# Weight chunks between two DMA queues, and the order of the first key matmuls, in a fused linear-attention and GeGLU kernel

## The chip, the cores and the metric

The kernel runs on one core of a Trainium2 chip. A time is the device time of one execution in microseconds, and the metric is the median over several executions; lower is better. The engines are named as in the profile: PE is TensorE (matmuls; PEld are its weight loads), DVE is VectorE, ACT is ScalarE, POOL is GpSimd and SP is SyncE, which here only issues DMAs. "SPq" and "ACTq" are instructions of SP's and ScalarE's queues that issue DMAs.

## What is computed

Two blocks work on the same input `x` (2048 rows of 640, bfloat16) and are mixed by a gate for each row. Block A is linear attention with 32 heads of 20, block B a GeGLU feed-forward net with 1728 hidden columns.

```python
g = sigmoid((x * gate_w).sum(-1, keepdims=True))
q, k, v = split(x @ wqkv)                      # 32 heads of 20 each
phi = lambda t: where(t > 0, t + 1, exp(t)) + 1e-6
pq, pk = phi(q), phi(k)
kv = einsum("bhsd,bhse->bhde", pk, v);  z = pk.sum(over s)
o = (pq @ kv) / (pq . z + 1e-6)
a = o @ wo
b = (gelu(x @ w_gate) * (x @ w_up)) @ w_down
out = g * a + (1 - g) * b
```

## The kernel before

**Tiling.** Rows are cut into 16 tiles of 128 and the 640 input columns into 5 chunks of 128 (`KC`). A product with a weight goes chunk by chunk: the transposed x tile (`xT[:, k, tile]`) is the stationary operand, the weight's chunk `k` the moving one, and 5 chunks add up in PSUM.

**Stages.** First come keys and queries of tiles 0 to 3 (`KM` at lines 445 to 458, `QM` at 460 to 473), with the feature map phi on ScalarE and VectorE behind them (`phi1`, `phi2`). Then come keys and queries of tiles 4 to 15 (`KQ`, line 532), then the sum over rows of phi(k) times x (`MM`, line 589), then the feed-forward net's first two products (`G`, line 689) with the attention's small products between them, and at the end the output tiles (`O_tile`, line 855).

**Who sets the order.** Every instruction goes through one planner (`P.op`), which appends it to its engine's list in program order and works out the semaphore waits from the tiles that it reads and writes. Each engine runs its list in order. Every load has a semaphore of its own. So the order of `KM` calls is TensorE's order, and the order of `load_...` calls is the order of issue on the queue that is named (`eng="sp"` unless said otherwise).

**The loads at the start.** Tile 0 of x is loaded as it is (`load_x(0)`) and transposed on TensorE by `T` (line 429), then copied by VectorE. Tiles 1 to 15 are transposed by the DMA itself (`load_xT`, line 352). The key weights come as five chunks of 160 KB (`load_wk`, line 349). Their issue on the two queues is:

| queue | order of issue at the start |
|---|---|
| SP | x tile 0, wk 0, transposed x tile 1, wk 3, wk 4, transposed x tiles 2 and 3, wq 0 to 4, transposed x tiles 4 to 15, then the bulk of x and the other weights |
| ScalarE | a tiny load (line 361), wk 1, wk 2, then the first Exp with its table load (line 372), then `gate_w` (line 374) |

**The first matmuls.** Warm-up matmuls on constants (`warm`, line 415) run until x tile 0 is there. Then tile 0 is transposed (lines 506 and 507), and the keys of tiles 0 and 1 are made chunk by chunk, alternating:

| step | what TensorE does (lines 509 to 517) |
|---|---|
| 1 to 3 | tile 0, chunks 0, 1, 2 |
| 4 to 6 | tile 1, chunks 0, 1, 2 |
| 7, 8 | tile 0, chunk 3; tile 1, chunk 3 |
| 9 | the gate column (`gate_col`, line 496): one small matmul of `gate_w` |
| 10, 11 | tile 0, chunk 4; tile 1, chunk 4 |

One step is two matmuls, 512 and 128 columns wide (lines 453 and 454). A step waits for its x tile and its weight chunk. Tiles 2 and 3 follow with all five chunks each (line 521), then the queries.

Of the kernel before, what the change touches and what calls it, by code (L numbers as in the profile page):

```python
# [162 lines left out]
def bass_gated_mix__linear_attn_block__geglu_ffn__prompt_kernel(  # L163
# [63 lines left out]
    with (  # L227
# [8 lines left out]
        with contextlib.ExitStack() as stack:  # L236
# [12 lines left out]
            def new_dma_key():  # L249
                k = "in%d" % dma_next[0]  # L250
                dma_next[0] += 1
                return k
# [16 lines left out]
            wk = wkq[:, :, 0:640]  # L269
# [40 lines left out]
            r_wk = [P.sb("wk%d" % k, R_WK + k * WW, R_WK + k * WW + 640) for k in range(KC)]  # L310
# [29 lines left out]
            def dma_in(dst, src, writes, reads=(), eng="sp"):  # L340
                P.op(eng, lambda e, dst=dst, src=src: e.dma_start(dst, src),
                     reads=reads, writes=writes, dma=new_dma_key())
# [3 lines left out]
            def load_x(i, eng="sp"):  # L346
                dma_in(x_aug[:, i, 0:640], A_x[0, i * 128:(i + 1) * 128, :], [r_xn[i]], eng=eng)

            def load_wk(k, eng="sp", after=()):
                dma_in(wk[:, k, :], A_wqkv[k * 128:(k + 1) * 128, 640:1280], [r_wk[k]], reads=after, eng=eng)  # L350

            def load_xT(i, after=()):
                P.op("sp", lambda e: e.dma_start_transpose(xT[:, :, i * 128:(i + 1) * 128],
                                                           A_x[0, i * 128:(i + 1) * 128, :]),
                     reads=list(after), writes=[r_xT[i]], dma=new_dma_key())

            def load_wq(k, eng="sp"):
# [4 lines left out]
                 writes=[P.res("touch")], dma=new_dma_key())  # L362
            load_x(0)
            load_wk(0)
            load_xT(1)
            load_wk(3)
            load_wk(4)
            load_wk(1, "act")
            load_wk(2, "act")

            zero = nc.const_aps.tensor(0.0, (128, 1), F32)
            P.op("act", lambda e: e.activation(eg[:, 0:1], zero, ACT.Exp), writes=[r_eg[0]])
# [15 lines left out]
            for c in range(NHC):  # L388
# [9 lines left out]
                 reads=[r_ones], writes=[r_ident])  # L398
# [16 lines left out]
            def warm(count, n):  # L415
                def fn(e):
                    last = None
                    for w in range(count):
                        last = e.matmul(ps[:, 4, 0:n], one_l, one_r[:, 0:n], start=True, stop=True)
                    return last  # L420
                P.op("pe", fn, writes=[bank[4]])
# [4 lines left out]
            def slot(n):  # L426
                return SLOTS[n % 4]
# [17 lines left out]
            def KM(n, ks):  # L445
                i = seq[n][1]
                b0, b1 = slot(n)

                def fn(e):
                    last = None  # L450
                    for k in ks:
                        lhs = xT[:, k, i * 128:(i + 1) * 128]
                        e.matmul(ps[:, b0, :], lhs, wk[:, k, 0:512], start=(k == 0), stop=(k == KC - 1))  # L453
                        last = e.matmul(ps[:, b1, 0:128], lhs, wk[:, k, 512:640],  # L454
                                        start=(k == 0), stop=(k == KC - 1))
                    return last
                P.op("pe", fn, reads=[r_xTa[i] if i < NXN and ks == [0] else r_xT[i]] + [r_wk[k] for k in ks],
                     writes=[bank[b0], bank[b1]])
# [37 lines left out]
            def gate_col():  # L496

                P.op("pe", lambda e: e.matmul(ps[:, 7, 0:5], gw_sb, ident[:, 0:5], start=True, stop=True),
                     reads=[r_gw, r_ident], writes=[bank[7]])
                P.op("dve", lambda e: e.tensor_copy(wq[:, :, 640:641], ps[:, 7, 0:5].unsqueeze(2)),  # L500
                     reads=[bank[7]], writes=[r_gcol])
# [4 lines left out]
            T(0, [0], 7)  # L506
            T(0, [1, 2, 3, 4], 6)
            warm(2, 128)
            for k in range(3):
                KM(0, [k])  # L510
            for k in range(3):
                KM(1, [k])
            KM(0, [3])
            KM(1, [3])
            gate_col()
            KM(0, [4])
            KM(1, [4])
# [48 lines left out]
            for i in range(NQ, NT):  # L566
                KQ(i)
                if i == 4:
                    late_constants()
            P.op("dve", lambda e: e.tensor_scalar(gg, eg, 0.5, 0.5, ALU.mult, ALU.add),  # L570
                 reads=r_eg, writes=[r_g])
            P.op("dve", lambda e: e.tensor_scalar(omg, eg, -0.5, 0.5, ALU.mult, ALU.add),
                 reads=r_eg, writes=[r_omg])
# [7 lines left out]
                 reads=[r_omg], writes=[r_od], dma=new_dma_key())  # L581
# [44 lines left out]
            def ME(g):  # L626
# [6 lines left out]
                for c in cs:  # L633
# [8 lines left out]
                 reads=r_pk[0:2], writes=[r_tmp[0]])  # L642
            for i in range(2, NT):
                P.op("dve", lambda e, i=i: e.tensor_tensor(zacc, zacc, pk[i], ALU.add),  # L644
                     reads=[r_tmp[0], r_pk[i]], writes=[r_tmp[0]])
# [283 lines left out]
```

## Time and profile before

| what | value |
|---|---|
| median of 7 executions | 273.81 us (273.47 to 275.66) |
| the profiled execution, its own time | 273.41 us |
| its span, first to last instruction | 272.1 us |
| TensorE's granted clock | 1.000 |
| PE busy in 0.8 to 3.2 us / 3.2 to 4.4 / 4.4 to 5.55 | 2.38 of 2.40 / 0.73 of 1.20 / 0.97 of 1.15 us |
| PE busy in 7.6 to 15.9 us / 15.9 to 48.4 | 8.30 of 8.30 / 32.50 of 32.50 us |
| PE busy in 48.4 to 80 us / 80 to 270 | 31.60 of 31.60 / 190.00 of 190.00 us |

The span is counted from the first instruction. The time of an execution is somewhat longer than its span, because it holds what lies before the first and behind the last instruction. The rows on PE come from a view that gives the busy time of each engine in chosen stretches. In that view a stretch is followed by its length and then by the busy time of PE, PEld, DVE, ACT and POOL, with the number of instructions in brackets. A group such as `L453 PE MATMUL ps<-pool` is the matmul of line 453 that reads SBUF (`pool`, the kernel's one large tensor there) and writes PSUM (`ps`).

### The profile page before, as it was taken

The numbers are of one execution on the slowest core, as the hardware profiler recorded it, in microseconds if no ns is written. First come the engines' busy times: TensorE is split into PE (matmuls) and PEld (weight loads), VectorE is DVE, ScalarE is ACT, GpSimd is POOL, SyncE is SP. The second block draws the span as 40 slices with busy tenths as digits, with TensorE's granted clock in tenths as the row PEclk, the third lists the DMA queues.
The fourth block names the chain that finished last, engine by engine and source line by source line (L and its number), as shares of the span: only waits on it lengthen the run. The fifth ranks groups of instructions, "written<-read, shape, count | busy, mean of one in ns | idle before, by whom it ended". The sixth has DMA issues, their size and how long they took to land.

```text
span 272.1 us, 3442 instructions
## 1 busy us (share of the span) xinstructions
PE 268.7 (99%) x1367; PEld 127.5 (47%) x1367; DVE 140.7 (52%) x247; ACT 75.9 (28%) x132; POOL 30.0 (11%) x28
## 2 busy tenths in 40 slices
PE   7999999999999999999999999999999999999997
PEld 3555555544445444444444444444444444444444
DVE  1689898997333335999999999634110000000200
ACT  2455555210422453322222232224012122121021
POOL 5000000004140002243332421000000000000000
PEclk9999999999999999999999999999999999999999
DMA  7876999600300011614121221272031110110211
GB/s 193 199 117 124 326 398 390 165 3 19 65 13 2 23 50 51 201 26 49 27 48 32 41 51 24 60 244 81 5 81 35 41 39 19 39 41 19 58 58 41
DMA packets 42864, 23.78 MB, mean 87 GB/s; under 512 B 32223, under 2 KB 41439, under 8 KB 42719
## 3 DMA queue, kind: packets, MB, share of 16 engines
q1 hardware_dynamic: 42517, 23.22, 31.8%
q10 hardware_dynamic: 330, 0.33, 0.3%
q8 instruction: 11, 0.18, 0.3%
q14 instruction: 6, 0.05, 0.1%
HBM read 13.83 MB, written 2.63 MB: 60 GB/s over the span
## 4 chain that ended last, share of the span: by engine, by line
PE 97%; DMA 1%; SPq 0%; DVE 0%; issue 0%
PE ps L700 41%; PE ps L864 23%; PE ps L539 12%; PE ps L596 6%; PE ps L843 4%; PE ps L468 2%; PE ps L811 2%; PE ps L678 2%; PE ps L599 1%; PE ps L453 1%; DMA pool<-in_A_x_dram 1%; PE ps L824 1%; PE ps L721 1%; PE ps L739 0%; PE ps L469 0%; PE ps L454 0%
## 5 line engine op out<-in xcount | busy, mean ns | idle before, releaser
L700 PE MATMUL ps<-pool 128*128 128x512 bf16 x520 | 113.7, 379 | 0.0
L700 PEld LDWEIGHTS ps<-pool 128*128 128x128 bf16 x520 | 50.5, 98 | 60.0
L864 PE MATMUL ps<-pool 128*128 128x512 bf16 (+2 forms) x306 | 62.7, 367 | 0.0
L706 ACT ACTIVATE pool<-ps 128x512 f32<-128x512 f32 x52 | 31.0, 597 | 73.1 <-PE ps L700 73.1
L708 DVE TENSOR_TENSOR pool<-ps,pool 128x512 bf16<-128x512 f32 x52 | 34.7, 690 | 31.7 <-PE ps L700 30.4
L864 PEld LDWEIGHTS ps<-pool 128*128 128x128 bf16 x306 | 29.2, 98 | 33.5 <-issue 0.4
L847 DVE TENSOR_TENSOR pool<-ps,pool 128x512 bf16<-128x512 f32 x4 | 2.8, 692 | 61.5 <-PE ps L843 61.5
L539 PE MATMUL ps<-pool 128*128 128x512 bf16 (+1 forms) x180 | 32.7, 344 | 0.0
L754 POOL TENSOR_TENSOR pool<-pool 128x640 f32<-128x640 bf16 x16 | 22.4, 1405 | 73.0 <-DVE pool L756 66.1
L871 ACT ACTIVATE pool<-ps,pool 128x512 bf16<-128x512 f32 (+1 forms) x16 | 10.9, 680 | 68.6 <-PE ps L864 68.6
L539 PEld LDWEIGHTS ps<-pool 128*128 128x128 bf16 x180 | 17.5, 98 | 15.0
L558 DVE SCALAR_TENSOR_TENSOR pool<-ps,pool 128x128 bf16<-128x128 f32 (+2 forms) x36 | 21.7, 602 | 2.1
L549 ACT ACTIVATE pool<-ps 128x640 bf16<-128x640 f32 x24 | 16.9, 703 | 15.8 <-DVE pool L558 9.3
L596 PE MATMUL ps<-pool 128*128 128x512 bf16 x78 | 19.4, 379 | 0.0
L764 DVE TENSOR_TENSOR pool<-pool 128x640 bf16<-128x640 bf16 x16 | 13.2, 826 | 0.6
L762 DVE TENSOR_SCALAR pool<-pool 128x32 f32<-128x32 f32 x16 | 12.8, 800 | 0.6
L756 DVE TENSOR_REDUCE pool<-pool 128x32 f32<-128x640 f32 x16 | 13.0, 809 | 0.0
L644 DVE TENSOR_TENSOR pool<-pool 128x640 f32<-128x640 f32 x14 | 11.6, 825 | 0.5
L843 PE MATMUL ps<-pool 128*128 128x512 bf16 x52 | 11.6, 380 | 0.0
L646 POOL PARTITION_ALL_REDUCE pool<-pool x1 | 4.0, 3972 | 60.4 <-DVE pool L644 60.4
L596 PEld LDWEIGHTS ps<-pool 128*128 128x128 bf16 x78 | 6.9, 98 | 7.3
L555 DVE TENSOR_SCALAR pool<-pool 128x640 bf16<-128x640 bf16 x24 | 7.9, 327 | 1.7 <-ACT pool L549 0.4
(70 smaller groups left out, 123.9 us busy)
## 6 DMA issues: line engine op xcount, KB each, us to landing
out_dram<-pool SPq DMA_DIRECT2D x19, 128.0 KB, 1.7
pool<-in_B_w_gate_dram SPq DMA_DIRECT2D x1, 2080.0 KB, 14.5
pool<-in_B_w_up_dram SPq DMA_DIRECT2D x1, 2080.0 KB, 17.7
pool<-in_A_wqkv_dram SPq DMA_DIRECT2D x8, 160.0 KB, 3.1
pool<-in_A_x_dram SPq DMA_DIRECT2D x1, 1280.0 KB, 9.5
pool<-in_A_x_dram SPq DMA_DIRECT2D x1, 1120.0 KB, 6.6
pool<-in_B_w_down_dram SPq DMA_DIRECT2D x1, 1120.0 KB, 6.1
pool<-omg_row SPq DMA_DIRECT2D x1, 1024.0 KB, 5.0
```

The source lines that it names most:

```text
L539: last = e.matmul(ps[:, b + p, 0:c1 - c0], xT[:, k, i * 128:(i + 1) * 128], wkq[:, k, c0:c1], start=(k == 0), stop=(k == KC - 1))
L549: P.op("act", lambda e: e.activation(e_buf[m], ps_flat[:, o:o + 640], ACT.Exp), reads=banks, writes=[r_e[m]])
L558: P.op("dve", lambda e, c0=c0, c1=c1: e.scalar_tensor_tensor(dst[:, c0:c1], ps_flat[:, o + c0:o + c1], 1.0 + EPS, e_buf[m][:, c0:c1], ALU. ...
L596: last = e.matmul(ps[:, b, :], pk[i][:, c * 128:(c + 1) * 128], x_aug[:, i, 0:512], start=(i == 0), stop=(i == NT - 1))
L700: last = e.matmul(ps[:, b, :], w[:, k, fc * 128:(fc + 1) * 128], xT[:, k, j * 512:(j + 1) * 512], start=(k == 0), stop=(k == KC - 1))
L706: P.op("act", lambda e: e.activation(ge[n], ps[:, gb, :], ACT.Gelu_apprx_tanh), reads=[bank[gb]], writes=[r_ge[n]])
L708: P.op("dve", lambda e: e.tensor_tensor(hT[fc][:, j * 512:(j + 1) * 512], ps[:, ub, :], ge[n], ALU.mult), reads=[bank[ub], r_ge[n]], write ...
L754: P.op("pool", lambda e: e.tensor_tensor(tmp[n], pq[i], z_b, ALU.mult), reads=[r_pq[i], r_zb], writes=[r_tmp[n]])
L756: P.op("dve", lambda e: e.tensor_reduce(den[n], tmp[n].rearrange("p (h d) -> p h d", h=32), AX.X, ALU.add), reads=[r_tmp[n]], writes=[r_de ...
L764: P.op("dve", lambda e: e.tensor_tensor(pq[i].rearrange("p (h d) -> p h d", h=32), pq[i].rearrange("p (h d) -> p h d", h=32), den[n].unsqu ...
L843: last = e.matmul(ps[:, b, :], wd[:, fc, 512:640], hT[fc][:, j * 512:(j + 1) * 512], start=False, stop=(fc == NFC - 2), skip_group_check=True)
L864: last = e.matmul(ps[:, pb, 0:c1 - c0], lhs, rhs, start=False, stop=(q == len(rows) - 1), skip_group_check=True)
```

## The change

Chunk 3 of the key weights is issued from ScalarE's queue, behind chunks 1 and 2, and no longer from SP's. On SP chunk 4 follows the transposed x tile 1, and the transposed tiles 2 and 3 follow chunk 4. TensorE makes tile 0's chunks 0 to 3 and then tile 1's chunks 0 to 3; the gate column and the two chunks 4 follow as before. The parameter `after` of `load_wk`, which no call used, goes.

```diff
-            def load_wk(k, eng="sp", after=()):
-                dma_in(wk[:, k, :], A_wqkv[k * 128:(k + 1) * 128, 640:1280], [r_wk[k]], reads=after, eng=eng)
+            def load_wk(k, eng="sp"):
+                dma_in(wk[:, k, :], A_wqkv[k * 128:(k + 1) * 128, 640:1280], [r_wk[k]], eng=eng)
...
             load_x(0)
             load_wk(0)
             load_xT(1)
-            load_wk(3)
             load_wk(4)
             load_wk(1, "act")
             load_wk(2, "act")
+            load_wk(3, "act")
...
             warm(2, 128)
-            for k in range(3):
+            for k in range(4):
                 KM(0, [k])
-            for k in range(3):
+            for k in range(4):
                 KM(1, [k])
-            KM(0, [3])
-            KM(1, [3])
             gate_col()
             KM(0, [4])
             KM(1, [4])
```

## The prediction

> **What bounds the kernel now.** I read four views, in this order: the busy line and the chain's summary, the waits of TensorE, TensorE's timeline between 4.4 and 7.7 us, and the transfers of that stretch.
>
> ```profile
> PE 268.7 (99%) x1367; PEld 127.5 (47%) x1367; DVE 140.7 (52%) x247; ACT 75.9 (28%) x132; POOL 30.0 (11%) x28
> PE 97%; DMA 1%; SPq 0%; DVE 0%; issue 0%
> ```
>
> TensorE is busy for 268.7 of 272.1 us. Only 3.4 us are not matmul, whatever their cause. The waits of TensorE over the whole run are three:
>
> ```profile
> PE ps L419 <- PEq L914: 0.8, 1, 0.8
> PE ps L453 <- DMA pool<-in_A_wqkv_dram: 0.5, 1, 0.5
> PE ps L453 <- DMA pool<-in_A_x_dram: 0.2, 1, 0.2
> ```
>
> The last two sit at the keys (line 453), where the change is. The columns are the sum, the number of times and the longest. The 0.8 us is the start of the program, and about 1.7 us at the end are the last store; the change reaches neither. The timeline (start, duration, instruction, idle before):
>
> ```profile
> 4.99 0.38 PE L453 MATMUL ps<-pool 128*128 128x512 bf16 x1
> 5.20 0.22 PE L454 MATMUL ps<-pool 128*128 128x128 bf16 x1
> 5.59 0.39 PE L453 MATMUL ps<-pool 128*128 128x512 bf16 x1 [0.17 <-DMA pool<-in_A_x_dram]
> ...
> 7.25 0.38 PE L453 MATMUL ps<-pool 128*128 128x512 bf16 x1
> 7.47 0.22 PE L454 MATMUL ps<-pool 128*128 128x128 bf16 x1
> 7.57 0.39 PE L453 MATMUL ps<-pool 128*128 128x512 bf16 x1
> ```
>
> A step (one 512-wide and one 128-wide matmul of one chunk) takes 0.27 us from start to start (4.72, 4.99). So tile 0 has used chunks 0 to 2 at 5.26, and the next step starts at 5.59: a hole of 0.33 us, ended by the transposed x tile 1. Seven steps and the gate matmul then lead to 7.52, and tile 2's first step starts at 7.57: a second hole of 0.05 us. From there on TensorE doesn't pause. So the change can win at most 0.33 + 0.05 = 0.38 us, 0.14% of the time.
>
> The chain of waits, and SP's and ScalarE's queues in that stretch:
>
> ```profile
> 1.71 3.83 DMA pool<-in_A_x_dram
> 5.54 0.05 issue
> 5.59 0.39 PE ps L453
> ```
>
> ```profile
> 1.71 1.30 SPq L353 DMA_TRANSPOSE pool<-in_A_x_dram  x1
> 3.06 1.04 SPq L341 DMA_DIRECT2D pool<-in_A_wqkv_dram  x2
> 4.14 2.53 SPq L353 DMA_TRANSPOSE pool<-in_A_x_dram  x2
> ```
>
> ```profile
> 1.24 0.93 ACTq L341 DMA_DIRECT2D pool<-in_A_wqkv_dram  x2
> 2.20 1.28 ACT L372 ACT_TABLE_LOAD   x1 [2.20 <-issue]
> 2.28 0.56 ACTq L341 DMA_DIRECT2D pool<-in_gate_w_dram  x1
> ```
>
> Tile 1 is complete at 1.71 + 3.83 = 5.54. Its issue isn't touched by the change, but what shares the DMA engines with it is. The table by stage (last columns: granted clock, DMA share, GB/s) says how full they are:
>
> ```profile
> 3.50:4.00 0.50, 0.43 (x6) 0.25 (x4) 0.36 (x2) 0.20 (x1) 0.50 (x1) 1.00 1.04 369
> 4.00:4.50 0.50, 0.05 (x1) 0.08 (x2) 0.27 (x1) 0.00 (x0) 0.36 (x3) 1.00 1.24 309
> 4.50:5.00 0.50, 0.50 (x5) 0.25 (x6) 0.00 (x0) 0.00 (x0) 0.20 (x1) 1.00 1.31 239
> 5.00:5.50 0.50, 0.42 (x4) 0.09 (x2) 0.00 (x0) 0.00 (x0) 0.00 (x0) 1.00 0.91 228
> 5.50:6.00 0.50, 0.41 (x3) 0.27 (x4) 0.00 (x0) 0.00 (x0) 0.00 (x0) 1.00 0.98 334
> ```
>
> The engines are full from 3.5 to 6.0 us: here a transfer can be sooner only at another's expense. In the DMA view of 4.1 to 5.0 us, queue 1 (SP's; it holds tile 1's transpose) has 682 packets and queue 10 (ScalarE's) only 47. Tile 1 now has the engines nearly to itself once wk chunks 1 and 2 are through.
>
> **What the skill says.** The Trainium skill's page "DMA: Bandwidth & Descriptors", section "Issuing engines are not separate DMA queues", has it that transfers started by ScalarE and SP run on the same 16 engines and interleave, so a second issuer saves only issue time. The trace agrees: between 2.75 and 4.1 us queue 10 took 61.3% of the engines' time and queue 1 32.5%, 94% together. Its section "Queues, rings and completion order" says that an engine takes turns between the queues packet by packet, and that each queue's ring is drained in order. The trace shows both queues moving in that stretch, but no large SP transpose beside a ScalarE load; how they share is my main unknown. "TensorE: Matmul & The Clock Gate", section "HAM oscillation — how this bites in real kernels", warns of idle gaps of about 3.4 us and more; the gap here is 0.33 us and the clock stands at 1.00 in all stages, so I cost the clock at nothing.
>
> **The change part by part.** Completion times below are the trace's completion stamps of the single transfers: wk1 4.49, wk2 4.90, gate_w 5.20, x tile 1 5.54, wk3 6.28, wk4 6.72, x tile 2 7.53, x tile 3 8.36.
>
> ScalarE's queue. wk3 is issued third, at about 2.17 (after 0.93 us for two, which began at 1.24), and takes 0.46 us. That moves gate_w's issue from 2.28 to 2.74 and its completion from 5.20 to some 5.65 (0.45 for wk3 ahead of it); the gate matmul starts at 6.96, so 1.3 us of cover remain. The table load and the first Exp move by as much and end at 4.15 instead of 3.69; ScalarE's next work is at 7.45. Both cost nothing; gone the cover, each would cost its excess.
>
> SP's queue. wk4 is issued at 3.06, tile 2's transpose at 3.67 instead of 4.14, and all behind it about 0.47 sooner (POOL's queue is not touched). wk4 comes earlier than 6.72 and is needed at about 7.1.
>
> Order on TensorE. Tile 0's chunk 3 stands before tile 1's chunk 0. No matmul is added; 0.27 us of work moves into the 0.33 us hole, if wk3 is there. It adds a wait: behind KM(0, [3]) all tile 1 steps, the gate and everything else queue in order.
>
> When wk3 lands. It follows wk2 on its ring; wk1 to wk2 was 0.41 us, so 4.90 + 0.41 = 5.31 at best. At worst it waits until tile 1 is through: its bytes are 163,840 at 369 GB/s = 0.44 us, so 5.54 + 0.44 = 5.98. As turns are taken and its packets are the larger (1,280 bytes against the transpose's 256 or so), I take 5.35.
>
> What that does to tile 1. Bounds: 0 (if it isn't limited by the engines) and 0.44 us (if wk3 goes ahead of its remaining packets). The shares of 1.24 and 1.31 say that packets queue, so I take 0.38: tile 1 at 5.92, its first step at 5.97. By then tile 0's chunk 3 (5.40 to 5.67) is done and no longer in the way.
>
> Sum. From tile 1's first step there remain six steps instead of seven, and the gate: 6 x 0.273 + 0.05 = 1.69, against 7.57 - 0.05 - 5.59 = 1.93 before. Tile 2 can start at 5.97 + 1.69 = 7.66, against 7.57: +0.09 us. With the bounds: delay 0.44 gives 7.72, +0.15; delay 0.3 gives 7.58, no difference.
>
> Tile 2. Sooner issued, it's still behind the same bytes: everything through tile 2 (x tile 0 and 1, five wk chunks, tile 2) is the same sum of bytes, on engines that are full until 6.0. The half us after 6.5 has a share of 0.64 only, so tile 2 can gain some 0.1 of it in the likely case, and up to its 0.47 of issue if the engines weren't what held it. In the likely case it lands before 7.6 and isn't waited for.
>
> Behind. Tile 3 lands at 8.36 and is needed at 7.57 + 5 x 0.273 = 8.94. The wq chunks come last at 12.25, against first use at 10.30 + 8 x 0.273 = 12.48; they are issued 0.47 sooner. No new wait there. What is 0.09 late at 7.6 is 0.09 late at the end, as TensorE has no hole to absorb it.
>
> The profiled execution is 273.41 us, 272.1 of span and 1.3 around it. 273.41 + 0.09 = 273.5. It lies 0.40 under the median of 273.81, and I carry that over: 273.9.
>
> **Rivals.**
> A, the likely case: 273.75 to 273.95; the hole is filled but tile 1 is late by about as much.
> B, it works as arranged: tile 1 stays at 5.54 because wk3 finds gaps, and tile 2 profits from its sooner issue. wk3 at 5.31: tile 0's chunk 3 runs from 5.36 to 5.63, then 5.63 + 1.69 = 7.32, a gain of 0.25 (up to 0.38 with both holes closed): 273.4 to 273.6. For it speaks that tile 1's packets start some time after its issue, so part of wk3 could pass ahead; against it, the full engines.
> C, wk3 is late: its wait holds up tile 1, which is there. With 5.98, seven steps and the gate remain: 5.98 + 0.05 + 1.96 = 7.99, +0.42: 274.2.
> D, the other side: as C, but wk3 doesn't get its turn before the second transpose either. It decides from wk3 at 6.39 on (6.39 + 2.01 = 8.40, +0.83); 6.5 gives +0.94: 274.75. For it: wk3 was at 6.28 on SP, and nothing in this trace shows ScalarE's third load beside a transpose. Against: it is issued 0.9 us sooner, and wk2, in the same place, took 3.2 us from issue to landing.
>
> **How the numbers follow.** A 0.58, B 0.20, C 0.12, D 0.10. About 0.3%, 0.82 us, is what a measurement of this kernel can tell from no change. A, B and C lie within it, B's best (0.38) too. The seven times reach from 273.47 to 275.66, so a median may fall over either bound by itself: I put 0.04 on faster and 0.12 on slower, nearly all of it D. The predicted time is A's, 273.9. The range reaches from B (273.3) to D's lower end (274.7).
>
> **What would show it.** Right: the matmul after tile 0's third step starts near 5.4 with no long wait; tile 1's first step starts at 5.9 to 6.0 on x; tile 2's at 7.55 to 7.7 without a wait; DMA share in 4.0 to 5.5 no lower than now, queue 10 with over 150 packets between 4.1 and 5.0. Wrong: tile 1's transpose still complete near 5.54 and tile 2 before 7.3 (B), or a wait on wqkv longer than 0.3 us after 5.26 (C, D), or any wait of TensorE after 7.7, which I exclude.

## The result, and the profile after

| | kernel before | changed kernel |
|---|---|---|
| median | 273.81 us (30 executions, 273.46 to 275.66) | 275.20 us (12 executions, 274.62 to 276.69) |
| ratio, 95% interval | | 1.0061 (1.0046 to 1.0075) |
| the profiled execution, its span | 273.41, 272.1 us | 276.63, 275.3 us |

The change costs 1.4 us in the median. The forecast was 273.9, no difference, and its range ended at 274.7. The waits of TensorE in the changed kernel (sum, times, longest):

```profile
PE ps L453 <- DMA pool<-in_A_wqkv_dram: 1.1, 1, 1.1
PE ps L419 <- PEq L912: 0.8, 1, 0.8
PE ps L453 <- DVE pool L437: 0.3, 1, 0.3
```

The wait for x tile 1 is gone, and a longer one for a weight chunk stands in its place. The timeline of TensorE shows where, and a second thing:

```profile
4.39 0.59 PE L453 MATMUL ps<-pool 128*128 128x512 bf16 x1 [0.34 <-DVE pool L437]
4.76 0.31 PE L454 MATMUL ps<-pool 128*128 128x128 bf16 x1
4.87 0.63 PE L453 MATMUL ps<-pool 128*128 128x512 bf16 x1
...
5.83 0.31 PE L454 MATMUL ps<-pool 128*128 128x128 bf16 x1
7.21 0.61 PE L453 MATMUL ps<-pool 128*128 128x512 bf16 x1 [1.06 <-DMA pool<-in_A_wqkv_dram]
7.61 0.31 PE L454 MATMUL ps<-pool 128*128 128x128 bf16 x1
7.71 0.63 PE L453 MATMUL ps<-pool 128*128 128x512 bf16 x1
...
10.35 0.38 PE L453 MATMUL ps<-pool 128*128 128x512 bf16 x1
10.57 0.22 PE L454 MATMUL ps<-pool 128*128 128x128 bf16 x1
10.62 0.38 PE L453 MATMUL ps<-pool 128*128 128x512 bf16 x1
```

Tile 0's fourth step starts at 7.21. From its start on, seven steps and the gate lead to tile 2, as they did from 5.59 on in the kernel before, so 1.62 us are lost up to here. Then the steps themselves: from 7.71 on they take 0.53 us from start to start, from 10.35 on 0.27. The three steps ahead of the hole were slow already (4.39, 4.87, 5.41). Tile 2 starts at 10.62 (the last line) and not at 7.57, 3.05 us later: 1.62 from waiting and 1.43 from slow steps. The profiled execution is 3.22 us above the profiled one of before, so the start explains nearly all of it. It is one of the four slowest of the 12 executions (276.26 to 276.69); the other eight lie between 274.62 and 275.29, about where the wait alone would put them (an estimate: 273.41 + 1.62 = 275.03).

The chain of waits names the transfer (start, duration):

```profile
2.17 0.03 issue
2.19 4.97 DMA pool<-in_A_wqkv_dram
7.16 0.05 issue
```

wk3, issued at 2.19 on ScalarE's queue, arrived at 7.16; on SP's queue it had arrived at 6.28 although it was issued at 3.06. Tile 1's transpose suffers with it. The DMA view of the stretch in which both are on their way (size, time from issue to completion):

```profile
pool<-in_A_wqkv_dram ACTq DMA_DIRECT2D x1, 160.0 KB, 5.0
pool<-in_A_x_dram SPq DMA_TRANSPOSE x1, 5.6
```

Tile 1 took 5.6 us instead of 3.8: it is complete at 7.33 and not at 5.54. The table by stage, last columns granted clock, DMA share and GB/s, answers to the table shown of before:

```profile
4.00:4.50 0.50, 0.16 (x2) 0.14 (x2) 0.30 (x1) 0.18 (x1) 0.36 (x3) 1.00 1.11 283
4.50:5.00 0.50, 0.50 (x3) 0.23 (x2) 0.00 (x0) 0.00 (x0) 0.20 (x1) 1.00 1.42 158
5.00:5.50 0.50, 0.50 (x4) 0.12 (x3) 0.00 (x0) 0.00 (x0) 0.00 (x0) 1.00 1.11 134
5.50:6.00 0.50, 0.50 (x4) 0.06 (x2) 0.00 (x0) 0.00 (x0) 0.00 (x0) 1.00 1.24 138
```

The engines are as full as before (shares above 1.1), but from 4.5 us on they move 134 to 158 GB/s where they moved 228 to 334. In the kernel before, transposes alone filled the engines at 238 GB/s (7.1 to 7.3 us, share 1.06, every packet under 512 bytes), and the stretch of nearly only ordinary loads, 3.5 to 4.0, moved 369. The new rate lies below both, so it isn't sharing: sharing would give a rate between the two. So there are two theories to test. M, mixing: a transposing transfer of one queue and an ordinary one of another slow each other down on the same engines. C, clock: the longer hole in TensorE's work keeps its matmuls slow or makes them slow again. The rivals are that the order of the matmuls costs the time, that the sooner issues on SP do, or that any two queues do this.

### The profile page after: what moved, and what is told of

Read it like the earlier page. It is cut to its first block, busy times and chain, and to the rows that moved or that the text cites. A ratio compares the mean times of both kernels' runs of the same rounds, so it can differ in the third digit from the quotient of the medians.

```text
span 275.3 us, 3442 instructions
## 1 busy us (share of the span) xinstructions
PE 271.2 (99%) x1367; PEld 128.4 (47%) x1367; DVE 140.6 (51%) x247; ACT 76.0 (28%) x132; POOL 30.0 (11%) x28
## 4 chain that ended last, share of the span: by engine, by line
PE 97%; DMA 2%; ACTq 0%; DVE 0%; issue 0%
PE ps L698 41%; PE ps L862 23%; PE ps L537 12%; PE ps L594 6%; PE ps L841 4%; PE ps L453 2%; DMA pool<-in_A_wqkv_dram 2%; PE ps L468 2%; PE ps L809 2%; PE ps L676 2%; PE ps L597 1%; PE ps L822 1%; PE ps L719 1%; PE ps L737 0%; PE ps L454 0%; PE ps L469 0%
## 5 line engine op out<-in xcount | busy, mean ns | idle before, releaser
L698 PE MATMUL ps<-pool 128*128 128x512 bf16 x520 | 113.7, 379 | 0.0
L594 PE MATMUL ps<-pool 128*128 128x512 bf16 x78 | 19.4, 379 | 0.0
L841 PE MATMUL ps<-pool 128*128 128x512 bf16 x52 | 11.6, 379 | 0.0
L453 PE MATMUL ps<-pool 128*128 128x512 bf16 x20 | 7.9, 485 | 1.4 <-DMA pool<-in_A_wqkv_dram 1.1
```

The source lines that it names most:

```text
L594: last = e.matmul(ps[:, b, :], pk[i][:, c * 128:(c + 1) * 128], x_aug[:, i, 0:512], start=(i == 0), stop=(i == NT - 1))
L698: last = e.matmul(ps[:, b, :], w[:, k, fc * 128:(fc + 1) * 128], xT[:, k, j * 512:(j + 1) * 512], start=(k == 0), stop=(k == KC - 1))
L841: last = e.matmul(ps[:, b, :], wd[:, fc, 512:640], hT[fc][:, j * 512:(j + 1) * 512], start=False, stop=(fc == NFC - 2), skip_group_check=True)
```

## The experiments

**The changed kernel again, twice.** A second profile beside the next three runs, and a third with timing beside a later series.

> The changed kernel once more, for a second profile. Theory M (mixing): while wk chunk 3 on ScalarE's queue and the transposed x tile 1 on SP's queue are in flight together, the DMA engines move both far below their usual rate; tile 1 is complete at about 7.3 us and wk3 at about 7.1 us again (before: 5.54 and 6.28), and tile 0's chunk 3 starts at about 7.2. Theory C (clock): the long hole then also delays the moment at which TensorE's matmuls go from 0.54 us a step to 0.27 us a step; when that happens differs from run to run, so that this profile shows the fast steps either from before 5 us (then about 275.0 us) or from about 10 us on (then about 276.6 us). A rival that the clock is only an accident of that one profile, and always late in this kernel, expects 276.6 again.

> The changed kernel beside the other three, on the same chip: 275.2 with executions between 274.6 and 277; tile 1 complete at 7.2 to 7.4 us, wk3 at 6.9 to 7.6.

Tile 1 was complete at 7.40 and 7.94, wk3 at 7.57 and 7.89. The times were 277.10 (one execution) and a median of 276.99 (13 executions, 274.79 to 278.25; ratio 1.0094, 1.0068 to 1.0119). In both profiles the first steps were fast, so the guess that a profile is either fast from 5 us or slow up to 10 us was too simple. TensorE's timeline of the third profile:

```profile
4.70 0.38 PE L453 MATMUL ps<-pool 128*128 128x512 bf16 x1
4.91 0.22 PE L454 MATMUL ps<-pool 128*128 128x128 bf16 x1
6.00 0.39 PE L453 MATMUL ps<-pool 128*128 128x512 bf16 x1 [0.87 <-DMA pool<-in_A_wqkv_dram]
6.23 0.22 PE L454 MATMUL ps<-pool 128*128 128x128 bf16 x1
7.94 0.61 PE L453 MATMUL ps<-pool 128*128 128x512 bf16 x1 [1.49 <-DMA pool<-in_A_wqkv_dram]
8.34 0.31 PE L454 MATMUL ps<-pool 128*128 128x128 bf16 x1
```

Before the second hole a 512-wide matmul takes 0.38 us, behind it 0.61; TensorE was fast once more at 11.5. The table by stage of this profile, with the granted clock third from the end, has it as a clock:

```profile
7.00:7.50 0.50, 0.00 (x0) 0.00 (x0) 0.00 (x0) 0.00 (x0) 0.00 (x0) 1.00 1.09 268
8.00:9.00 1.00, 1.00 (x5) 0.45 (x6) 0.00 (x0) 0.00 (x0) 0.00 (x0) 0.50 1.24 316
11.50:12.00 0.50, 0.50 (x5) 0.29 (x4) 0.00 (x0) 0.50 (x2) 0.00 (x0) 1.00 0.96 213
```

The clock fell to one half at about 8.0 us, behind holes of 0.87 and 1.49 us close together, and rose at about 11.4. The second profile shows the same from 7.6 to 11.0, behind a wait of 0.79 us, some steps and a hole of 1.52. The first one reads 1.00 throughout although its steps were slow until 10.3, so in this view 1.00 doesn't prove fast steps.

**Order alone.** The queues of before, the new order of the matmuls:

```diff
-            for k in range(3):
+            for k in range(4):
                 KM(0, [k])
-            for k in range(3):
+            for k in range(4):
                 KM(1, [k])
-            KM(0, [3])
-            KM(1, [3])
```

> Only the order of the matmuls is changed, the queues are those of before. Theory M: tile 1 is complete at 5.5 us and wk3 at 6.3 us as before; tile 0's chunk 3 starts at 6.33 and holds up tile 1; seven steps and the gate remain, so tile 2 starts at 8.3 instead of 7.57: +0.7 us over before, 274.5, and more if the hole of 1.1 us makes the clock late. Rival (the order itself costs the whole 1.4 us): 275.2. Rival (order is harmless): 273.8.

274.19 us, 22 executions, against 274.01 of before beside it: ratio 1.0011 (0.9996 to 1.0027). The transfers were as before (tile 1 at 5.62, wk3 at 6.44), and tile 2 started at 8.43. The cost was smaller than expected: no difference that can be measured. A second profile of before, below, suggests why. Fast steps stayed fast here behind a hole of 0.97 us:

```profile
6.49 0.39 PE L453 MATMUL ps<-pool 128*128 128x512 bf16 x1 [0.97 <-DMA pool<-in_A_wqkv_dram]
```

**Queues alone.** The changed loads, the old order (the reverse of the diff above, made to the changed kernel).

> Only the queues are changed, the order of the matmuls is that of before. Theory M: the transfers are as in the changed kernel, tile 1 complete at about 7.3 us, so tile 1's first step starts at about 7.35 with seven steps to go, against 7.2 with seven steps to go in the changed kernel: 275.2 to 275.4, as slow as the whole change. Rival (the wait of tile 0's chunk 3 in front of tile 1 is what costs): tile 1 comes first again and the time is about that of before, 273.8 to 274.0.

276.55 us, 10 executions (274.84 to 278.5): ratio 1.0092 (1.0059 to 1.0125). Tile 1 was complete at 7.31, wk3 at 7.11. TensorE's waits in it:

```profile
PE ps L453 <- DMA pool<-in_A_wqkv_dram: 0.8, 1, 0.8
PE ps L453 <- DMA pool<-in_A_x_dram: 0.7, 1, 0.7
```

The first wait is for the weights of tile 0's first step, the second is the hole: with the old order TensorE waits for tile 1 instead of wk3, to the same effect. So the loads cost the time, and the order doesn't save it. The median lies above the forecast. In the profile (277.79 us) the steps took 0.53 us from the first one to about 12.2, which would explain it; the other executions weren't traced.

**The same loads with an ordinary tile 1.** In the changed kernel and in the kernel before:

```diff
-            load_xT(1)
+            P.op("sp", lambda e: e.dma_start(xT[:, :, 128:256],
+                                             A_x[0, 128:256, :].rearrange("s (k p) -> s k p", k=KC)),
+                 writes=[r_xT[1]], dma=new_dma_key())
```

> The changed kernel, but x tile 1 is loaded by an ordinary copy in pieces of 256 bytes into the same place instead of by a transposing DMA (the transpose of that tile is left out, so the keys and queries of tile 1 are of other numbers). Theory M, in the form that a transposing and an ordinary transfer disturb each other: with no transpose in flight until tile 2's, wk3 is complete at about 5.3 us and tile 1 by about 5.9, ordinary packets of 1,280 bytes keep their 55 ns, and the first hole of TensorE almost goes. Rival (small packets and large packets of two queues disturb each other, whatever they are): tile 1 and wk3 come after 7 us as in the changed kernel. Rival (ScalarE's third load is slow by itself): wk3 after 7 us, tile 1 in time.

> The kernel before, with x tile 1 loaded by an ordinary copy in 256-byte pieces (its transpose is left out). The fourth corner: with wk3 on ScalarE the copied tile came at 6.31 us and the transposed one at 7.2 to 7.9; with wk3 on SP the transposed one comes at 5.5 to 5.6. Theory M (transpose and ordinary loads disturb each other beyond sharing): the copied tile at 5.7 to 5.9, so wk3 costs it the 0.44 us of its own bytes and not 1.8. Rival (the copied tile suffers as much from wk3): 4.7 or sooner.

The copied tile (size, time from issue to completion), first in the changed kernel, then in the kernel before:

```profile
pool<-in_A_x_dram SPq DMA_DIRECT2D x1, 160.0 KB, 4.6
```

```profile
pool<-in_A_x_dram SPq DMA_DIRECT2D x1, 160.0 KB, 4.0
```

With both, the table has its four corners (when tile 1 was complete, one number for each profile; it is issued at 1.71 or 1.72 in all):

| tile 1 | wk3 on SP, behind it | wk3 on ScalarE, beside it | wk3 costs it |
|---|---|---|---|
| transposing DMA | 5.54, 5.62, 5.71, 5.77 | 6.92, 7.18, 7.31, 7.33, 7.40, 7.94 | 1.2 to 2.4 us |
| ordinary copy in 256-byte pieces | 5.68 | 6.31 | 0.63 us |

wk3 was complete at 6.16 with the copy beside it. Tile 1 and wk3 came later there than forecast (5.9 and 5.3), but not after 7 us as in the changed kernel. Each of the two copies is one profile. About 0.6 us of the delay is thus what an ordinary neighbour costs too, a little more than the 0.44 us worked out from wk3's bytes; the rest, 0.6 to 1.7 us if the four transposes without a neighbour are averaged to 5.66, came only with a transpose. The times of the two single executions were 274.27 and 274.18. The DMA view from 4.3 to 6.1 us shows it in the packets (packets, MB, share of 16 engines). First the changed kernel, then the one with the copied tile:

```profile
q10 hardware_dynamic: 111, 0.13, 66.4%
q1 hardware_dynamic: 522, 0.15, 55.8%
```

```profile
q1 hardware_dynamic: 1063, 0.40, 83.4%
q10 hardware_dynamic: 174, 0.18, 28.2%
```

An average packet of queue 10 took 66.4% x 16 x 1.8 us / 111 = 172 ns of an engine's time beside the transpose, and 28.2% x 16 x 1.8 / 174 = 47 ns beside the copy. The whole rate was 155 GB/s against 321.

**Half of wk3.**

```diff
+            load_half(1, "sp")
             load_wk(4)
...
-            load_wk(3, "act")
+            load_half(0, "act")
```

`load_half(h, eng)` loads 64 of the chunk's 128 rows, and the steps with chunk 3 wait for both halves.

> wk3 is cut in two by rows: 64 rows go by ScalarE's queue as in the changed kernel, 64 by SP's behind tile 1's transpose. Theory M, each ordinary packet beside a transpose costing some 200 ns of an engine instead of 55: 4 packets on each engine instead of 8, so about half of the 1.8 us: tile 1 complete at 6.3 to 6.6 us. Rival (any ordinary load in flight slows the transpose as a whole): 7.3 us. Rival (plain sharing by bytes): 5.75 us.

Tile 1 at 6.30 us, as forecast. The delay grows with the load beside the transpose (0.76 us for 64 packets, 1.79 for 128, against the first profile of before; one profile of the half); it isn't a switch that one neighbour throws. The reason given in the forecast doesn't hold, though. A row of the table by stage, and the packets of ScalarE's queue from 4.7 to 5.3 us, in which this half was moved:

```profile
5.00:5.50 0.50, 0.50 (x4) 0.23 (x3) 0.00 (x0) 0.00 (x0) 0.00 (x0) 1.00 1.15 299
```

```profile
q10 hardware_dynamic: 84, 0.08, 40.1%
```

That is 40.1% x 16 x 0.6 us / 84 = 46 ns for a packet and not some 200, at 299 GB/s and not 134. Tile 1 was late all the same, so slow packets of the neighbour are not the whole of what delays a transpose. The time of the one execution was 274.97; it waits for the half on SP, at 6.91.

**wk3 later.** Its issue waits for tile 1:

```diff
-            load_wk(3, "act")
+            load_wk(3, "act", [r_xT[1]])
```

> wk3 stays on ScalarE's queue and the order is that of the changed kernel, but its issue waits until x tile 1 is complete. Theory M: tile 1 is complete at 5.5 to 5.7 us again, as in the kernel before, since nothing of wk3 is in flight beside it; wk3 then runs into tile 2's transpose and comes at 8 us or later, so the time is 275.5 or more, slower than the changed kernel. Rival (the sooner issue of wk4 and of tiles 2 and 3 on SP is what delays tile 1): tile 1 at 7.3 us still.

279.58 us (4 executions): ratio 1.0193 (1.0161 to 1.0226). Tile 1 is complete at 5.56 again, with wk4 and the next transposes issued as soon as in the changed kernel; the sooner issues on SP are not the cause. wk3, issued at 5.58, now meets the transpose of tile 3 and the end of tile 2's. The DMA view of 5.6 to 5.9 us and the table by stage:

```profile
pool<-in_A_wqkv_dram ACTq DMA_DIRECT2D x1, 160.0 KB, 4.0
pool<-in_A_x_dram SPq DMA_TRANSPOSE x1, 4.9
```

```profile
7.50:8.00 0.50, 0.00 (x0) 0.00 (x0) 0.00 (x0) 0.00 (x0) 0.00 (x0) 1.00 1.33 149
8.00:8.50 0.50, 0.00 (x0) 0.00 (x0) 0.00 (x0) 0.00 (x0) 0.00 (x0) 1.00 1.29 149
```

The same signature in another place: a share of 1.3 at 149 GB/s. The load needs 4.0 us and tile 3's transpose 4.9, against 3.0 in the kernel before. The profiled execution (280.41) also shows the price of a long hole, here of 3.88 us: the granted clock is 0.50 from about 8.7 to 15.6. Of the 7.0 us over the profiled execution of before, 4.0 are the wait (9.57 + 2.01 against 7.57) and 3.0 the slow steps (half of 9.6 to 15.6).

**wk3 out of the way.** The first attempt left a wait in place: tile 0's chunk 3 still waited for the late load, so its time says nothing on the question.

> The changed kernel with wk3 out of the way: chunk 3's keys of tiles 0 to 3 are made with chunk 2's weights (so they are of other numbers), and chunk 3 is loaded on SP behind the queries' weights for the later tiles. Theory M: tile 1 complete at 5.5 us, tile 0's fourth step fills the hole at 5.26 to 5.53, and tile 2's first step starts at 7.2 to 7.3 us if its transpose comes by then: 0.3 us under the kernel before. So what the arrangement could win, with transfers at no cost, is about 0.3 us, against the 1.4 us that it lost. Rival (the sooner issue on SP also delays): tile 1 after 6 us and no gain.

It took 282.03 us; tile 1 came at 5.93. The second attempt waits for chunk 2 only (`r_wk[2 if k == 3 else k]`):

> As the run before it that left wk3 out of the way, but without its wait: chunk 3's keys of tiles 0 to 3 are made with chunk 2's weights and wait for those only. Theory M: with no wk3 beside it tile 1 is complete at 5.5 to 5.9 us (it was 5.93 with the same loads), tile 0's fourth step fills the hole, tile 2's first step starts at 7.3 to 7.6 us: 273.5 to 273.8, at most 0.3 under the kernel before. Rival (the order or the sooner issue on SP costs too): 274.2 or more.

273.63 us, 22 executions, beside 273.95 of before: ratio 0.9992 (0.9977 to 1.0008). Without wk3 beside tile 1 the loss is gone. The median is 0.32 us lower, about what the forecast allowed, but the interval doesn't tell it from nothing, so a gain isn't shown. In the profile (274.00, not one of the faster executions) tile 1 is complete at 5.86 and no hole is left, yet tile 2 starts at 8.14 and not at 7.3 to 7.6, because the first three steps were slow ones.

**Filling the hole.** First five, then more warm-up matmuls on constants in the changed kernel. The second edit:

```diff
-            warm(2, 128)
-            for k in range(4):
+            warm(2, 512)
+            for k in range(3):
                 KM(0, [k])
+            warm(7, 512)
+            KM(0, [3])
```

> The changed kernel with five more 512-wide warm-up matmuls on constants between tile 0's chunks 2 and 3, where TensorE waits. Transfers as in the changed kernel. Theory C: they keep TensorE busy through most of the hole, so the steps after it take 0.27 us; the executions near 276.6 us disappear, and the median falls to 274.9 to 275.1, what the late transfers alone cost (+1.2). If the steps before them are slow, they take 5 x 0.43 = 2.1 us and end at about 8 us, which costs up to 0.8 us there. Rival (the clock is not steered by the hole): the spread stays at 274.6 to 276.7 and the median at 275.2 or above.

> The changed kernel with more work on constants: the two warm-up matmuls ahead of the keys are 512 wide instead of 128, and seven more 512-wide ones stand in the hole between tile 0's chunks 2 and 3. Theory C: TensorE is then busy nearly without a pause from the start, so the fast steps begin before the hole in every execution: no execution above 275.8, median 274.9 to 275.2 against 275.2 of the changed kernel beside it, whose executions near 276.6 remain. Rival (those executions come from transfers that are late in them): the spread stays as wide as that of the changed kernel.

With five: 275.09 us (21 executions, 274.54 to 277.2), ratio 1.0046 (1.0030 to 1.0062); three executions were still above 276, so this fill doesn't settle it. With the longer fill: 275.40 us (13 executions, 275.03 to 275.88), ratio 1.0044 (1.0030 to 1.0059). The third run of the changed kernel stood beside it on the same chip: median 276.99, up to 278.25, nine of 13 above 276. The median expected for the fill was a little low, because its matmuls hold TensorE until 7.86, behind wk3 (6.78); but the spread is gone, with tile 1 still late (6.92). In TensorE's timeline of it the first step behind the fill is fast:

```profile
6.33 1.70 PE L419 MATMUL ps<-const-bfloat16-1.0 128*128 128x512 bf16 x7
...
7.86 0.38 PE L453 MATMUL ps<-pool 128*128 128x512 bf16 x1
...
8.13 0.38 PE L453 MATMUL ps<-pool 128*128 128x512 bf16 x1
```

Theory C holds: more matmuls in the program took 1.6 us off the median of that series. Earlier transfers don't explain it: in this profile tile 0's fourth step starts at 7.86, in the third one of the changed kernel at 7.94, but tile 2 starts at 9.79 and at 11.54, and the two executions differ by 1.8 us.

**The kernel before again.**

> The kernel before once more, for a second profile; its first one was faster (273.41) than the median of its executions (273.8 to 274.0). Expected if that difference lies at the start: a time near 273.9 and tile 2's first step at about 8.0 us instead of 7.57, because the loads came some tenths later or because the first steps were slow ones of 0.54 us. Rival (the difference lies elsewhere): 7.6 us again.

273.95 us, and TensorE's timeline has a longer hole in front of tile 2 than the first profile had (0.05 us):

```profile
7.48 0.38 PE L453 MATMUL ps<-pool 128*128 128x512 bf16 x1
...
7.70 0.22 PE L454 MATMUL ps<-pool 128*128 128x128 bf16 x1
...
8.11 0.39 PE L453 MATMUL ps<-pool 128*128 128x512 bf16 x1 [0.19 <-DMA pool<-in_A_x_dram]
```

Tile 2 starts at 8.11, 0.36 us after the last step would allow (7.48 + 0.27), since its transpose was complete at 8.06. That fits the small cost of order alone, 0.2: its tile 2 at 8.43 is 0.32 behind this one, not 0.86 behind the first profile. Measured from this one, the changed kernel's wait with fast steps costs 7.21 + 1.98 - 8.11 = 1.08 us. One more profile is one more sample; how 8.1 and 7.6 are spread isn't known.

**Two versions that might beat both.** One loads x tile 1 as it is and transposes it on TensorE (`NXN = 2`, `load_x(1)` in place of `load_xT(1)`, and two calls `T(1, [0], 5)` and `T(1, [1, 2, 3, 4], 3)`), so that no transposing DMA stands among the first loads. The other is the kernel before with `warm(2, 512)` in place of `warm(2, 128)` and a `warm(1, 512)` behind tile 0's chunk 2.

> A version of the kernel before without a transposing DMA among the first loads: x tile 1 is loaded as it is, directly behind tile 0, and transposed on TensorE as tile 0 is (5 small matmuls and two copies of VectorE more). Theory M: only ordinary loads run until about 5 us, all chunks come at the full rate (wk3 by 5.4, wk4 by 5.9), the five transposes lie in the idle time at 4 us, tile 0's first step starts at about 4.7 and no hole follows; ten steps and the gate take 2.8 us, so tile 2 starts at about 7.5 or, if its transpose is late, when that comes: 273.3 to 273.8, same or up to 0.4 faster than before. Rival (the added transposes and copies cost more than the hole): 274.2.

> The kernel before with the two warm-up matmuls ahead of the keys 512 wide instead of 128, and one more in the hole between tile 0's chunk 2 and tile 1's chunk 0. Theory C: the fast steps begin earlier in the executions where they are late; those above 275 disappear (6 of 58 before), and the median falls by 0 to 0.3 us. Rival (the added matmuls are in the way): median 0.2 to 0.4 above before.

The first: 275.50 us (22 executions, 273.93 to 276.56), ratio 1.0040 (1.0021 to 1.0058). The loads were not slowed as beside a transpose, but came 0.3 to 0.5 us later than expected (wk3 at 5.89, wk4 at 6.21), and tile 0's first step started at 5.42 and not at 4.7, as it stands behind tile 1's transposes and VectorE's copies. Its profile is of its fastest execution (273.93); slow steps would fit the others, but no trace of those was taken. The second: 273.88 against 273.84, ratio 1.0000 (0.9991 to 1.0008); no execution above 275 fell into either side of that series, so it shows neither gain nor cost. Neither beats the kernel before.

## Why the prediction was wrong

**What was right.** The holes of the profiled execution and their causes; that little could be won (the run without wk3 was 0.32 us lower, not told from nothing); the issue times (wk3 at 2.19, wk4 at 3.07, tile 2 at 3.68, the first Exp ended at 4.17); that what is late at tile 2 is late at the end; no wait of TensorE behind 7.7 us. The formula of case D holds too: wk3's completion plus 2.01 is when tile 2 starts at fast steps. Order alone shows it (6.44 + 2.01 = 8.45, measured 8.43), and in the changed kernel 7.16 + 2.01 = 9.17 would be 1.60 late.

**The step that failed: "What that does to tile 1. Bounds: 0 ... and 0.44 us".** The upper bound, and with it the value of 0.38, came from wk3's bytes at the engines' rate of 369 GB/s, that is from the assumption that two transfers share a constant rate. Measured: 1.79 in the profile, 1.2 to 2.4 over six profiles with these loads. The same assumption put wk3 at 5.35, "at worst" 5.98; it came at 7.16. Tile 1 as an ordinary copy lost 0.63 to the same neighbour. The table of before already had a hint: from 5.0 to 5.25 us the engines have only ordinary packets, wk3's behind tile 1's transpose, and 47 of them at a share of 119.2% took 101 ns each on average; its 5.00 to 5.50 row moves 228 GB/s at 0.91, while the row of 3.5 to 4.0, nearly all ordinary loads, moves 369 at 1.04. I read the share as a queue and didn't ask why a full engine moved less.

**The second: "I cost the clock at nothing".** It rested on a gap of 0.33 us in the kernel before, against the 3.4 us of which the Trainium skill's page "TensorE: Matmul & The Clock Gate" warns ("HAM oscillation — how this bites in real kernels"). In the second and third profile fast steps became slow behind holes of 1.5 us, less than half of that figure, each with another pause of 0.8 to 0.9 us shortly before; behind holes of 0.97 us (order alone) and 1.08 us (half of wk3) they stayed fast. In the first profile the steps hadn't become fast at all before the hole. It was a cost that hung on another step's being right, and it should have been priced for case D. In the profiled execution it is 1.43 of 3.05 us.

**The chances.** D, the slower case, had 0.10, and its own example stood at 274.75. It had the direction, but not the reason: wk3 didn't wait for its turn behind a second transpose, its packets were moving beside tile 1's, slowly, from about 4.5 us on. What I held against it was wk2, "in the same place", with 3.2 us; but only wk2's last packets met the first of tile 1's, between 4.0 and 4.4, and there the engines still moved 309 GB/s. gate_w, third behind wk3, came at 7.54 and not at 5.65, wk4 at 7.73 and not before 6.72; both lay beside the same wait and cost nothing more.

**What stays open.** Why a transpose and an ordinary load of two queues slow each other: the runs show that they do, and not by what mechanism. Two facts an explanation has to meet: the first half microsecond in which both moved didn't lose rate (4.0 to 4.5 us in the changed kernel, 283 GB/s), and half of wk3 delayed the transpose without being slow itself. How often the steps stay slow differs between series (4 of 12 executions of the changed kernel above 276 us in one, 9 of 13 in another); what decides that wasn't found.

## What to carry to other kernels

A load moved to another queue isn't only issued sooner: it runs beside other transfers than before, and next to a transposing DMA it cost here up to four times what its bytes account for (1.79 us against 0.44). In the table by stage read DMA share and GB/s together, and compare the rate with what each kind of transfer moves alone; a full share at a rate below both was interference here and not load. And where TensorE's first steps wait for data, price a longer wait twice: once as the wait, once as slow matmuls behind it.

## What the runs showed of the hardware

- Packets of ScalarE's queue, most of them of 1,280 bytes, took 172 ns of an engine on average beside a transposing DMA of SP's queue, and 47 ns beside an ordinary copy of the same tile in 256-byte pieces; the total rate was 155 GB/s against 321.
- Half of that load delayed the transpose by 0.76 us, though its own packets took 46 ns.
- The Trainium skill's page "DMA: Bandwidth & Descriptors", section "Issuing engines are not separate DMA queues", says that a second issuer saves only the time of issue. Here it also changed which packets meet: the same 160 KB behind the transpose, on its queue, left it at 5.54 us, and beside it, on the other, put it at 7.33. The measurement decides.
- Matmul steps doubled, from 0.27 to 0.53 us, behind holes of 0.87 and 1.49 us close together, and the granted clock read 0.50 from 8.0 to 11.4 us; behind one hole of 0.97 us they didn't. The clock stayed at 0.50 for about 3.4 us in two profiles, 6.8 us behind a hole of 3.88 us.
- Where the steps were slow from the first one on (the first profile of the changed kernel, until 10.3 us), the granted clock in the table by stage read 1.00; there only the durations show it.
